# A state-space and MLP block on one core: eight buffers for X, the table spread on VectorE, some normalisations on GpSimd, and a new order of work

## The chip, the core and the metric

The kernel runs on one core of a Trainium2 chip. The metric is the device time of one execution in microseconds (us). A core has five engines with a queue each: TensorE (PE in the profile; its weight loads are PEld), VectorE (DVE), ScalarE (ACT), GpSimd (POOL) and SyncE (SP), which here only starts transfers (DMA). Each engine works through its own instructions in the order in which the program lists them, and waits on semaphores for the others.

## The reference

Sequence 2048, width 512, bf16. Two kinds of layers alternate, A, B, A, B, with the same weights in both rounds:

```python
x = A_q
x = x + A(layernorm(x))      # A: q * y
x = x + B(layernorm(x))      # B normalises its input once more
x = x + A(layernorm(x))
x = x + B(layernorm(x))

# A: k_shift = causal 4-tap filter of k along the sequence; kv = k_shift * v
#    y = long convolution of kv with ssm_k (length 2048, by FFT) + kv * ssm_D
#    result q * y, where q is the normalised x
# B: y = layernorm(x); h = gelu_tanh(y @ w1 + b1); result h @ w2 + b2    (512 -> 1376 -> 512)
```

The convolution's result y depends on k, v and the filter alone, so it is the same in both A layers and is computed once.

## The kernel before

The work falls into two parts. **The front part** computes y as a transform in two stages, written as matmuls with tables, on tiles of 1024 PSUM columns (two banks each):

- *ht*: the filter is loaded in four blocks of 128 channels (512 KB each) and transposed on TensorE, four tiles of 16 transposes, each copied from PSUM to SBUF. ssm_D is added into the first row of each of the four (line 521, VectorE or GpSimd).
- *s2*: a table that comes from memory in two halves (512 KB each) is spread to four times its size by eight multiplications with masks (lines 498 to 503), 128x2048 each. h2 and x2 read the result.
- *h1* and *h2*: the filter's first and second stage, 16 tiles each (lines 534 and 547). h2 needs all of h1. Its result H lies in SBUF, the core's memory, and 16 transfers of 256 KB (line 564) put a copy with exchanged partition halves beside it, HS.
- *fir*: k, brought in by eight transposing transfers, is filtered on TensorE (line 584, 8 tiles) and multiplied with v on VectorE (line 590).
- *x1*, *x2*: the same two stages for kv. x1 has 16 tiles. x2 (`products`, line 598) runs for two halves of the channels, `PARTS`, eight tiles for each half: TensorE's tile of 16 matmuls, a copy of it to a buffer of X in SBUF (line 615), and a multiplication of X with H and HS on VectorE (line 618, 128x2048) that overwrites H and HS.
- *i1*, *i2*: the way back. i1 has 8 tiles for each half (line 634) and needs all eight products of its half; i2 has 5 tiles for each half (line 688) and leaves y.

X has four buffers of 1024 columns, used in turn (lines 612 and 613), in the memory `R_7`, where the transposed k lay before, so that the first of them waits for the last reader of k. The same memory later holds eight buffers for normalised slices (`ntmp`, line 727).

**The back part** works on the sequence in 16 slices of 128 rows, gathered in blocks: in the first round 1, 1, 2, 2, 2, 2, 2, 2, 2 slices (blocks 0 to 8), in the second 4, 4, 4, 4. For each block:

- statistics of each slice on VectorE (line 709, then the aggregate in line 711), a power on GpSimd for the inverse deviation (lines 715 and 717), the first normalisation (`norm`, line 723), the multiplication with y and the addition to x (lines 750 and 751; in the first four slices in two halves of 256 columns);
- the same statistics again, and a second normalisation;
- a transposition of the normalised slice: for slices 0 and 1 of the first round on TensorE (line 769), for all others by a transposing transfer on SP (line 762); the transposed block has two buffers in turn;
- m1, eleven tiles of four matmuls (line 782) and a gelu on ScalarE (line 787); m2, eleven matmuls per slice (line 815, in three groups of 4, 4 and 3), added to x on VectorE (line 819). In the second round the results are stored to memory as they become ready; the last slice is done in three pieces (lines 804 to 810).

**The order** of all this is written out. The program records 1082 operations by their dependences. `ORDER` lists them in the sequence in which they are given to the engines, so that each engine's own sequence is what `ORDER` leaves of it. `SECOND` names those that run on the second of two engines they may run on: copies from PSUM are on ScalarE or VectorE (`BOTH = (ACT, DVE)`), the row adds of ht on VectorE or GpSimd. `BANKS` gives the PSUM banks of each tile. `sync` sets the semaphore waits from the dependences. In the kernel before, VectorE has 357 operations, ScalarE 222, GpSimd 70, SP 89; of the eight spreads seven are on VectorE and one on ScalarE; of the 96 copies from PSUM (front part and transposes of slices 0 and 1) 23 are on VectorE.

Of the kernel before, what the change touches and what calls it, by code (L numbers as in the profile page):

```python
# [7 lines left out]
ALU = mybir.AluOpType  # L8
AF = mybir.ActivationFunctionType
# [3 lines left out]
PE, ACT, DVE, POOL, SP = "tensor", "scalar", "vector", "gpsimd", "sync"  # L13
# [25 lines left out]
class Prog:  # L39
# [48 lines left out]
    SECOND = (  # L88
        31, 32, 33, 34, 35, 36, 37, 43, 46, 47, 49, 50, 53, 55, 67, 75, 77, 79, 81, 89, 99, 101, 107, 109, 139, 143, 165, 175, 183, 209,
        257, 259, 360)  # L90
    BANKS = (
# [7 lines left out]

    def __init__(self, nc):  # L100
        self.nc = nc
# [259 lines left out]
PARTS = ((0, 64), (64, 64))  # L361
# [494 lines left out]
```

## Time and profile before

| | us |
|---|---|
| median of 3 runs | 242.53 (242.35 to 243.30) |
| the profiled execution | 241.77 |
| its span, first to last instruction | 240.0 |
| TensorE busy | 227.0 (95%) |
| VectorE busy | 177.8 (74%) |
| ScalarE busy | 141.1 (59%) |
| GpSimd busy | 33.2 (14%) |

The span and all times inside the kernel are of the one profiled execution, counted from its first instruction. A busy share is an average over parts of the kernel with different limits. Matmuls overlap with one another, so that TensorE's busy time is longer than the sum of what each costs in a dense row: 16 matmuls of x1 start 0.447 us before those of the next tile. The granted clock of TensorE is 1.0 throughout.

In a group's line stand line number, engine, operation, output and input with shapes, count, then busy time and mean ns of one, then the idle time of the engine before them. A timeline line has start, length, engine, line and operation. In a line of the chain of waits: start, length, and the work that the end waited for at that time.

### The profile page before, as it was taken

Reading aid. Unit: us, or ns where it says so; the run is one execution under the profiler, and the core shown is the slowest. Engines: PE = TensorE matmul, PEld = TensorE weight load, DVE = VectorE, ACT = ScalarE, POOL = GpSimd, SP = SyncE. Lnnn points to the kernel's source line nnn. Section 1 sums busy time; section 2 is a strip of 40 time slices with the busy share of each in tenths; the row PEclk is TensorE's granted clock in tenths of the full one; section 3 lists DMA queues with packets and bytes.
Section 4 is the critical chain, followed back from the end, with each engine's and each line's share of the span. In section 5 each row is a group of like instructions: output and inputs, shape, how many; then the busy total and the mean of one; then the engine's idle time right before and its main releaser. Section 6 shows DMA issues by size and latency. Waiting matters only on the chain.

```text
span 240.0 us, 5685 instructions
## 1 busy us (share of the span) xinstructions
PE 227.0 (95%) x2403; PEld 153.5 (64%) x2418; DVE 177.8 (74%) x357; ACT 141.1 (59%) x220; POOL 33.2 (14%) x74
## 2 busy tenths in 40 slices
PE   6897999888999799999999999999999999999995
PEld 2786889777899686767465856754444444444444
DVE  0899899999998999999899999999979231022013
ACT  2698749999989993739334726627406603703810
POOL 1160000100032224133213022030210100000000
PEclk9999999999999999999999999999999999999999
DMA  6999928999910013020601123122062141002002
GB/s 215 335 262 276 183 72 262 288 317 331 391 45 3 0 27 63 6 44 0 90 0 22 25 44 67 25 45 45 19 78 80 22 109 45 2 0 87 0 3 87
DMA packets 41582, 24.09 MB, mean 100 GB/s; under 512 B 27762, under 2 KB 37844, under 8 KB 41556
## 3 DMA queue, kind: packets, MB, share of 16 engines
q1 hardware_dynamic: 40738, 23.57, 37.3%
q8 instruction: 19, 0.31, 0.6%
q10 hardware_dynamic: 818, 0.15, 0.5%
q14 instruction: 7, 0.06, 0.1%
HBM read 11.40 MB, written 2.10 MB: 56 GB/s over the span
## 4 chain that ended last, share of the span: by engine, by line
PE 75%; ACT 9%; DVE 7%; DMA 4%; issue 1%; POOL 1%; SPq 1%
PE ps L815 30%; PE ps L782 30%; ACT ar L450 9%; PE ps L632 6%; DMA ar<-in_A_ssm_k_dram 3%; PE ps L582 3%; PE ps L545 3%; DVE ar L450 3%; PE ps L804 1%; DMA ar<-ar 1%; DVE sm L709 1%; PE ps L686 1%; DVE ar L447 1%; DVE ar L503 1%; SPq L436 1%
## 5 line engine op out<-in xcount | busy, mean ns | idle before, releaser
L787 ACT ACTIVATE ar<-ps,sm 128x256 bf16<-128x256 f32 (+3 forms) x143 | 68.5, 532 | 73.5 <-PE ps L782 73.4
L782 PE MATMUL ps<-ar 128*128 128x256 bf16 (+5 forms) x569 | 81.5, 297 | 1.3 <-ACT ar L787 1.1
L815 PE MATMUL ps<-ar 128*128 128x512 bf16 (+1 forms) x329 | 76.3, 379 | 0.6
L450 ACT ACTIVATE ar<-ps 128x1024 bf16<-128x1024 f32 (+2 forms) x73 | 67.3, 1035 | 11.7 <-PE ps L515 4.2
L782 PEld LDWEIGHTS ps<-ar 128*128 128x128 bf16 (+1 forms) x572 | 53.1, 100 | 28.9 <-DVE sm L709 1.3
L815 PEld LDWEIGHTS ps<-ar 128*128 128x128 bf16 (+1 forms) x341 | 33.3, 98 | 36.7 <-ACT ar L787 0.4
L819 DVE TENSOR_TENSOR ar<-ar,ps 128x512 bf16<-128x512 bf16 x31 | 21.0, 678 | 39.7 <-PE ps L815 39.7
L447 DVE TENSOR_TENSOR ar<-ar 128x512 bf16<-128x512 bf16 (+3 forms) x89 | 46.5, 536 | 2.4 <-ACT ar L450 0.9
L709 DVE BATCH_NORM_STATS2 sm<-ar 128x6 f32<-128x512 bf16 (+1 forms) x68 | 43.2, 649 | 0.9
L723 DVE TENSOR_SCALAR ar<-ar,sm 128x512 bf16<-128x512 bf16 x64 | 24.5, 412 | 5.8 <-POOL sm L717 4.2
L450 DVE CAST ar<-ps 128x1024 bf16<-128x1024 f32 x19 | 22.7, 1213 | 0.4 <-PE ps L545 0.2
L715 POOL TENSOR_SCALAR sm<-sm 128x2 f32<-128x2 f32 (+2 forms) x26 | 5.3, 204 | 116.3 <-DVE sm L711 115.8
L717 POOL TENSOR_TENSOR sm<-sm 128x2 f32<-128x2 f32 (+2 forms) x26 | 20.6, 793 | 2.2
L532 PE MATMUL ps<-ar 128*64 128x128 bf16 x512 | 17.2, 221 | 1.5 <-ACT ar L450 1.0
L532 PEld LDWEIGHTS ps<-ar 128*64 128x64 bf16 x512 | 14.8, 110 | 3.4 <-ACT ar L450 2.0
L632 PE MATMUL ps<-ar 128*128 128x128 bf16 x256 | 15.2, 220 | 0.6 <-ACT ar L450 0.6
L632 PEld LDWEIGHTS ps<-ar 128*128 128x128 bf16 x256 | 14.6, 114 | 0.9 <-ACT ar L450 0.9
L711 DVE BATCH_NORM_AGGREGATE sm<-sm 128x2 f32<-128x6 f32 (+1 forms) x64 | 11.3, 180 | 1.6
L609 PE MATMUL ps<-ar 128*128 128x64 bf16 x256 | 10.9, 199 | 1.7 <-ACT ar L450 1.7
L609 PEld LDWEIGHTS ps<-ar 128*128 128x128 bf16 x256 | 9.6, 118 | 2.9 <-ACT ar L450 2.6
L589 DVE TENSOR_TENSOR ar<-ps,ar 128x1024 bf16<-128x1024 f32 x8 | 9.5, 1220 | 1.1 <-PE ps L582 1.0
L545 PE MATMUL ps<-ar 128*128 128x128 bf16 x128 | 8.7, 221 | 1.3 <-DVE ar L450 1.3
(31 smaller groups left out, 79.1 us busy)
## 6 DMA issues: line engine op xcount, KB each, us to landing
ar<-ar SPq DMA_DIRECT2D x16, 256.0 KB, 5.4
ar<-in_A_ssm_k_dram SPq DMA_DIRECT2D x4, 512.0 KB, 6.4
ar<-in_A_v_dram SPq DMA_DIRECT2D x4, 512.0 KB, 4.6
ar<-in_A_q_dram SPq DMA_DIRECT2D x4, 512.0 KB, 5.4
out_dram<-ar SPq DMA_DIRECT2D x7, 256.0 KB, 2.0
ar<-in_B_w_dram SPq DMA_DIRECT2D x1, 1376.0 KB, 11.9
ar<-in_B_w_dram SPq DMA_DIRECT2D x1, 1280.0 KB, 9.9
ar<-tab_s SPq DMA_DIRECT2D x2, 512.0 KB, 6.5
```

The lines of the kernel that those rows point to most:

```text
L447: return P.op(eng, lambda e: e.tensor_tensor(o, a, b, op), reads=[a, b] + list(more), writes=[o])
L450: f = {ACT: lambda e: e.activation(dst, src(), AF.Copy), DVE: lambda e: e.tensor_copy(dst, src())}
L532: r = e.matmul(Q(tl, 64 * ri, 64, i * 128, [1, 128]), w, m, start=True, stop=True)
L609: r = e.matmul(Q(tl, 0, 128, i * pitch, [1, n]), w, m, start=True, stop=True)
L632: r = e.matmul(Q(tl, 0, 128, i * 128, [1, 128]), w, m, start=q == 0, stop=q == 1)
L709: P.op(DVE, lambda e, sj=sj, x=x: e.bn_stats(sj, x), reads=[x], writes=[sj])
L717: P.op(POOL, lambda e: e.tensor_tensor(r, v, hf, ALU.pow), reads=[v, hf], writes=[r])
L723: P.op(DVE, lambda e: e.tensor_scalar(o, x, m, r, ALU.subtract, ALU.mult), reads=[x, m, r], writes=[o])
L782: r = e.matmul(Q(tl, 0, rows, 0, [1, w]), a, m, start=dk == 0, stop=dk == 3)
L787: P.op(ACT, lambda e, dst=dst, tl=tl, rows=rows, bias=bias, w=w: e.activation(dst, Q(tl, 0, rows, 0, [1, w]), AF.Gelu_apprx_tanh, bias=bia ...
L815: r = e.matmul(Q(tl, 0, 128, 0, [1, 512]), ins[fc][0], ins[fc][1], start=fc == 0, stop=fc == 10)
L819: P.op(DVE, lambda e, x=x, tl=tl: e.tensor_tensor(x, x, Q(tl, 0, 128, 0, [1, 512]), ALU.add), reads=[x], writes=[x], tile=tl)
```

## The change

No operation is added or taken away. Four things change:

1. *X.* Each half has eight buffers of its own, one for each tile, so that none is used twice: the first half's lie in `R_4`, where the filter's first stage (read by h2) lay and later i1's result lies; the second half's in `R_5`, where kv (read by x1) lay and later y lies. X no longer shares memory with the transposed k. `R_7` keeps the transposed k and then the normalised slices.
2. *The spread.* All eight multiplications may run on VectorE alone.
3. *First normalisations of the first round* may run on VectorE or GpSimd. Eight of the 18 are put on GpSimd: those of slices 0 and 1, both of block 2, and one each of blocks 4, 5, 7 and 8.
4. *The order.* `ORDER`, `SECOND` and `BANKS` are replaced as a whole. VectorE now has 350 operations, GpSimd 77, ScalarE 222, SP 89. Copies from PSUM on VectorE: 22 instead of 23; all four of ht, four of h1, four of h2, five of x1, none of x2, three of i1, one of i2, one of the slices' transposes. On SP the four blocks of the filter come first, then the two halves of the table, then k, v and the rest. On TensorE the tiles of m1 and m2 of neighbouring blocks are mixed more than before, and the last twelve groups of matmuls belong to seven slices of the last two blocks.

```diff
     ORDER = (
-        0, 4, 24, 23, 27, 1, 7, 20, 28, 2, 6, 5, 12, 21, 10, 29, 11, 42, 38, 16, 43, 13, 51, 8, 52, 44, 31, 54, 56, 32, 17, 55, 9, 48, 30,
...
+        7, 0, 27, 28, 2, 22, 1, 51, 24, 4, 6, 42, 52, 53, 43, 29, 48, 49, 80, 44, 81, 84, 60, 85, 5, 20, 50, 72, 73, 32, 21, 30, 34, 8, 274,
...
     SECOND = (
-        31, 32, 33, 34, 35, 36, 37, 43, 46, 47, 49, 50, 53, 55, 67, 75, 77, 79, 81, 89, 99, 101, 107, 109, 139, 143, 165, 175, 183, 209,
-        257, 259, 360)
+        43, 44, 46, 49, 52, 53, 61, 65, 67, 69, 87, 93, 113, 115, 139, 141, 143, 163, 165, 251, 253, 261, 292, 305, 348, 360, 393, 398, 503,
+        555, 662, 714)
...
-    R_XB, R_N = R_7, R_7
+    R_N = R_7
+    XB = {PARTS[0][0]: R_4, PARTS[1][0]: R_5}
...
-            P.op(BOTH, {ACT: lambda e, o=o, x=x, w=w: e.activation(o, x, AF.Copy, scale=w),
-                        DVE: lambda e, o=o, x=x, w=w: e.tensor_scalar(o, x, w, None, ALU.mult)}, reads=[x, w], writes=[o])
+            P.op(DVE, lambda e, o=o, x=x, w=w: e.tensor_scalar(o, x, w, None, ALU.mult), reads=[x, w], writes=[o])
...
-            xo = R_XB + (nx[0] % 4) * 1024
-            nx[0] += 1
+            xo = XB[d0] + k0 // nk * 1024
...
-    def norm(s, mr, o):
+    def norm(s, mr, o, eng=DVE):
         x = A(0, 128, R_X + s * 512, [1, 512])
         m, r = mr
-        P.op(DVE, lambda e: e.tensor_scalar(o, x, m, r, ALU.subtract, ALU.mult), reads=[x, m, r], writes=[o])
+        P.op(eng, lambda e: e.tensor_scalar(o, x, m, r, ALU.subtract, ALU.mult), reads=[x, m, r], writes=[o])
...
-                norm(s, mr[i], zt)
+                norm(s, mr[i], zt, DVE if L else (DVE, POOL))
```

96 rows, old and new, of tables (BANKS, ORDER) are left out of this document.

## The prediction

> **What bounds it now.** I read four views in this order: the busy time by stage, the chain that ended last, the groups by shape, and the timeline of one collision. By stage (stretch and its length, then busy us and count on TensorE, its weight loads, VectorE, ScalarE and GpSimd; granted clock, DMA share, GB/s):
>
> ```profile
> 21.40:43.20 21.80, 21.42 (x480) 19.24 (x480) 20.30 (x19) 16.21 (x18) 0.29 (x2) 1.00 0.80 197
> 43.20:61.60 18.40, 15.78 (x368) 13.77 (x368) 18.21 (x20) 18.40 (x22) 0.76 (x2) 1.00 1.06 322
> 61.60:79.40 17.80, 17.80 (x271) 17.14 (x272) 16.73 (x34) 16.63 (x20) 4.29 (x11) 1.00 0.29 113
> 79.40:89.80 10.40, 8.58 (x116) 7.13 (x115) 9.69 (x33) 10.08 (x26) 2.33 (x6) 1.00 0.07 14
> 89.80:237.60 147.80, 147.00 (x843) 83.48 (x856) 98.30 (x240) 65.36 (x125) 19.76 (x37) 1.00 0.19 40
> ```
>
> Up to 43 us TensorE has enough to do, to 61.6 ScalarE is never idle and VectorE hardly, then TensorE again, then a gap at 79 to 90, and from 90 us TensorE is full to the end at full clock. So time can be won only before 90 us, and lost anywhere. The chain says the same (start, length, what):
>
> ```profile
> 17.95 3.40 DVE ar L450 x3
> ...
> 37.61 12.48 ACT ar L450 x14
> ...
> 69.55 5.36 PE ps L632 x96
> ...
> 87.35 2.45 DMA ar<-ar
> ...
> 89.84 2.54 PE ps L815 x11
> ```
>
> First VectorE, then ScalarE copying PSUM, then i1 on TensorE, then the transposing DMA behind a second normalisation, and after it matmuls alone.
>
> Prices by shape (busy, mean ns of one), and the one collision of GpSimd with a normalisation:
>
> ```profile
> L503 DVE TENSOR_SCALAR ar<-ar,sm 128x2048 bf16<-128x2048 bf16 x7 | 5.1, 769 | 0.2 <-DMA ar<-tab_s 0.2
> ...
> L502 ACT ACTIVATE ar<-ar,sm 128x2048 bf16<-128x2048 bf16 x1 | 2.0, 1993 | 0.0
> ...
> L447 POOL TENSOR_TENSOR ar<-ar 128x256 bf16<-128x256 bf16 x4 | 2.8, 696 | 6.2 <-DMA ar<-in_A_shift_k_dram 6.0
> ```
>
> ```profile
> 70.34 0.80 DVE L723 TENSOR_SCALAR ar<-ar,sm 128x512 bf16<-128x512 bf16 x1
> 70.47 0.52 POOL L668 MEMSET ar<- 1x512 bf16 x1
> ```
>
> Sums below use start-to-start spacing in dense stretches of the timeline, which is shorter than the mean duration because neighbours overlap: on VectorE 1.135 us for a 1024-column PSUM copy or a product of X, 0.62 for statistics over 512 columns, 0.14 for their aggregate, 0.33 for a normalisation, 0.43 for a 512-wide add or multiply, 0.66 for a spread; on ScalarE 0.91 for a PSUM copy. TensorE: 0.447 us per tile of h1, x1 and h2, 0.893 per tile of i1, 0.216 per 512-column matmul.
>
> **Start (0 to 21.5 us).** First h2 matmul: now at 21.46. The new order puts the four filter loads ahead of both tables. Now they land at 5.27, 6.58, 9.54 and 10.95 with a table between the second and third; without it the last two move up one slot each, to about 8.2 and 9.5, and the tables to about 11 and 12.4. VectorE then has ahead of the last h1 copy: four transposed-filter copies (4 x 1.15), two row adds (2 x 0.2), five spreads (5 x 0.66) and four h1 copies (4 x 1.135), in all 12.8 us after 6.57, plus about 1 us of waits for the second table and the last transposes: 20.4. ScalarE has lost its spread (1.9) and one filter copy (1.8) and got two more h1 copies (+1.8); its twelve end at about 20.7. First h2 at about 20.9, 0.6 earlier. But three spreads now stand behind the h1 copies (3 x 0.66, to 22.4), and the fourth h2 tile in the new order needs them: it would be ready at 22.2. With the copies behind it, the seventh h2 tile ends near 24.3 and the first fir tile near 25.3, where it ends now (25.25). Worth: nothing at the end of it, bounds -0.6 and +0.3.
>
> **Up to i1 of the second half.** Last fir product: now ends at 38.2; in the new order, with all h2 ahead of the last fir tile, at 39.5 (TensorE: 25.3 plus 9 h2, 7 fir at 0.87, 2 x1 and ten changes of tile shape at the 0.2 us seen now, 38.3; then the product's 1.2). From there to the last product of the second half VectorE has, now, 6 copies, 16 products, 4 statistics, 2 aggregates, a normalisation: 28.1, to 66.3, measured 66.7. New: 5 copies, 16 products, 4 statistics, 4 aggregates: 26.9, to 66.4, with 0.2 of waits 66.6. First i1 tile of that half: 67.1 now, 66.9 then. **Eight buffers** remove a wait that this trace does not show: ScalarE, which fills them, is busy all 18.40 us of the second row, so nothing waited for a fifth buffer. I cost them at 0; the cover is that VectorE's products set the pace, and if they did not, ScalarE's 0.91 against VectorE's 1.135 for eight tiles is 1.8 us at most. R_5 and R_4 are free of their old readers by then (all x1, all h2 done in TensorE's own order). On SP one swap that the second half of the first products needs stands behind fifteen other transfers; issued near 44.6 and landing 2.7 later it is there at 47.3, wanted at 49. That is 1.7 us of cover.
>
> **The gap at 79 to 90 and behind it** decides. From the last product to the last second normalisation of block 4, VectorE has now 17 normalisations, 19 statistics (8 half wide), 16 aggregates, 25 adds and multiplies (16 half wide), 3 copies and small ones: 30.2 us. In the new order: 12 normalisations (five now on GpSimd), 25 statistics, 19 aggregates, 28 adds and multiplies, one i2 copy more: 34.6. The five save 1.6; six statistics (3.7), three multiplies (1.3), three aggregates (0.4) and the copy (0.6) are new before this point. TensorE's work between first i1 of the second half and first m1 of block 4 is 34.7 now and 35.6 then, two m1 tiles more. Measured now: 66.7 + 30.2 = 96.9, but that normalisation ended at 99.7, so 2.8 us are waits (for i2, for GpSimd's powers, for dependent neighbours). TensorE reached block 4 at 105.0 where 67.1 + 34.7 = 101.8: 3.2 idle. New, with the same 2.8: 66.6 + 34.6 + 2.8 = 104.0, DMA 2.45 as in the chain: 106.4. TensorE would be there at 66.9 + 35.6 = 102.5, so 3.9 idle. What comes after is the same work, so the end moves by (66.9 + 3.9) - (67.1 + 3.2) = **+0.5**. Blocks 5 to 8 and the second layer have 0.7 us or more between landing and need by the same sums.
>
> **Normalisations on GpSimd.** No row shows one. From below 0.19 (its tiny TENSOR_SCALAR, in the timeline); nearest, 0.61 for a two-input op over 256 columns undisturbed; from above 2 x 0.94, twice the slowest of those four, which ran beside a spread. On GpSimd's own queue the statistics of block 2 stand behind one and those of block 4 behind another; each has over 2 us to spare, so the length alone costs 0. What it does to VectorE: the normalisation in the last fence took 0.80 instead of 0.41 beside a 0.52 us GpSimd write, 0.39 lost; multiplies beside GpSimd's powers stayed at 0.42. So 0 to 0.94 (the slowest row again) lost for each; I take 0.39, the row of a normalisation. Six of the eight fall before block 4's deadline; two lie beside copies and statistics, one beside m2 adds; three beside products, normalisations and multiplies. 3 x 0.39 = 1.2, less 0.2 slack: **+1.0**, bounds 0 and 5.6.
>
> The Trainium skill (SBUF — State Buffer, "SBUF: two separate sides") says that the port pair that VectorE and GpSimd share is an exclusive lock for a whole instruction and the loser blocks entirely; the 0.39 of 0.52 fits it. Its GPSIMD Engine Reference (3.1) has 769 ns for 512 elements of a tight loop; by that, as an estimate, three blocked instructions would cost 2.3 in place of 1.2.
>
> **Tail.** Now the last matmul ends at 237.58 and the kernel at 240.0. New: four adds of 0.6 to 0.69 fall within TensorE's last 1.3 us, and a 256 KB store (2.0 to landing) goes out after one of them in place of a 32 KB one (1.5). **+0.2**, bounds 0 and 0.6.
>
> Sum 0.5 + 1.0 + 0.2 = +1.7: span 240.0 to 241.7. The profiled execution took 241.77 against a median of 242.53, 0.8 apart; the median moves to **244.2**.
>
> **Rivals.** (1) *Faster.* The added statistics fill VectorE's 2.8 us of waits in place of standing behind them, and GpSimd hinders nobody. Then block 4 is normalised at 101.2, lands at 103.7, and TensorE's idle time is set by blocks 0 and 1. Block 0's i2 copy ends near 77.2, as now (77.3); from there to its transposes it is 2.8 now, one multiply more then: 80.4. Block 1's normalisation follows 1.9 later, its transposes and their copy take 1.5 more: first m1 at 83.9, where TensorE's own work gives 82.1. So 1.8 in place of 3.2. -1.4 - 0.2 + 0.2: 241.1. For it: VectorE idled 0.76 at 77.4 and 0.7 us in the row of the gap. Against: most waits are links of one chain, statistics, power, normalisation, DMA, which other work doesn't shorten. It decides when block 4's data land before 104.3. (2) *The lock in full:* all six GpSimd normalisations stop VectorE for their length, 0.61 each: 3.7 - 0.2 + 0.5 + 0.2 = +4.2: 246.7. For it the collision above; against, copies from PSUM beside GpSimd kept 1.21. (3) *No collision matters, the rest holds:* +0.7: 243.2.
>
> **Chances.** Forecast 0.36, rival 1 0.30, rival 3 0.22, rival 2 0.12. Range 240.3 to 247.2: rival 1 less 0.8, rival 2 plus 0.5; the forecast's own range is 243.2 to 245.4. Half a per cent (1.2 us: below 241.3, above 243.7) is about what can be told from no change. Faster: 0.24 of rival 1 and 0.01 of rival 3, 0.25. Slower: 0.25 of the forecast, 0.04 of rival 3, all of rival 2, 0.41. Same: 0.34.
>
> **What would show it.** First h2 near 20.9 with a wait at the fourth tile; first i1 of the second half near 66.9; first m1 of block 4 waiting for its DMA near 106; products or multiplies lengthened beside GpSimd's 512-wide TENSOR_SCALAR; TensorE full after that. Wrong if i1 of the second half begins before 65.5, if block 4 doesn't wait, or if TensorE idles after 110 us.

## The result and the profile after

| | before | after |
|---|---|---|
| median, us | 242.69 (242.35 to 243.3, 4 runs) | 245.13 (244.97 to 246.0, 4 runs) |
| ratio after to before | | 1.0125, 95% interval 1.0098 to 1.0152 |
| profiled execution, us | 241.77 | 246.0 |
| its span, us | 240.0 | 244.2 |

The changed kernel is slower by about 1.25%, 2.4 us by the medians and 3.0 by the ratio, where the forecast said 0.6 to 0.7%. The profiled execution is the longest of its four; the spans of the other three are 243.2 to 243.4 us. Line numbers after the change are lower by one (norm 722, powers 714 and 716, products 448, copies 451). Operations are named by their numbers in `ORDER`.

Busy time by stage, cut at the first i1 tile of the second half and the first m1 tile of block 4 (stretch, length, then busy us and count of TensorE, weight loads, VectorE, ScalarE, GpSimd; clock, DMA share, GB/s). The kernel before:

```profile
21.40:67.10 45.70, 42.70 (x944) 38.51 (x944) 43.98 (x44) 40.11 (x44) 1.05 (x4) 1.00 0.92 266
67.10:105.04 37.94, 36.03 (x396) 29.05 (x395) 35.16 (x97) 28.71 (x57) 12.09 (x27) 1.00 0.11 24
105.04:237.60 132.56, 131.85 (x741) 73.21 (x752) 84.09 (x203) 57.87 (x107) 14.29 (x26) 1.00 0.18 40
```

and the changed one:

```profile
21.10:69.90 48.80, 42.64 (x944) 38.42 (x944) 44.10 (x45) 42.39 (x47) 18.49 (x11) 1.00 0.89 262
69.90:109.10 39.20, 37.44 (x403) 29.45 (x404) 36.12 (x99) 29.30 (x59) 17.32 (x27) 1.00 0.11 22
109.10:241.30 132.20, 131.70 (x744) 72.15 (x744) 76.28 (x193) 52.30 (x105) 18.59 (x28) 1.00 0.18 37
```

TensorE has the same 944 matmuls in the first stretch and as much busy time, but the stretch is 3.1 us longer. The second is 1.3 longer, with seven matmul records and 1.4 us of TensorE's busy time more, and the third is 0.4 shorter. (Block 4's first matmul starts at 105.25 before and 109.08 after, its first weight load at 105.04 and 109.08; cut at the matmul the second stretch is 1.0 longer.) Most of what is lost is lost before 70 us, where GpSimd is busy 18.5 us instead of 1.1. The chain that ended last (start, length, what) says what the first stretch waited for:

```profile
20.96 6.33 DMA ar<-in_A_v_dram
34.33 2.37 DVE ar L589 x2
...
47.76 9.28 ACT ar L451 x10
...
62.62 7.21 DVE ar L448 x6
69.97 2.85 PE ps L631 x48
...
106.58 2.45 DMA ar<-ar
```

A transfer of v is now one of its longest links; the chain of the kernel before has none. VectorE's waits in the first stage (who, for what: us in all, times, longest), in the kernel before:

```profile
DVE ar L589 <- PE ps L582: 1.0, 3, 0.4
DVE ar L450 <- PE ps L545: 0.2, 1, 0.2
DVE ar L447 <- ACT ar L450: 0.2, 1, 0.2
```

and in the changed one between 20 and 70 us, with GpSimd's below them:

```profile
DVE ar L589 <- DMA ar<-in_A_v_dram: 2.0, 1, 2.0
...
DVE ar L448 <- ACT ar L451: 0.9, 1, 0.9
```

```profile
POOL sm L662 <- DMA ar<-in_B_b_dram: 6.9, 1, 6.9
```

The 2.0 us stand ahead of the first filter product (135), for the v rows of transfer 16, landed at 27.30. Not all of them are the transfer's: the filter tile that 135 also needs ended at 26.00. The 0.9 are put down to ScalarE, which had long been done; what landed then, at 51.23, is swap 126 (one of the transfers that make HS), and product 199, the second of the second transform stage, starts at 51.31. The 6.9 us are GpSimd's: a copy of ten columns of the gelu biases (276) stands at the head of its queue until transfer 275 has landed at 50.60. Behind it are the powers of blocks 0 and 1 and their normalisations.

In the kernel before, 276 stood ahead of the same powers and waited for 275 even longer, but there 275 landed at 40.97, ahead of block 0's statistics, so that it held up nothing. GpSimd in the kernel before:

```profile
41.02 0.19 POOL L663 CAST sm<-ar 128x10 f32<-128x10 bf16 x1 [23.81 <-DMA ar<-in_B_b_dram]
...
43.84 0.19 POOL L715 TENSOR_SCALAR sm<-sm 128x1 f32<-128x1 f32 x1 [2.47 <-DVE sm L711]
```

What moved is the transfer. SP issues it behind 33 others where it was behind 23, at 46.10 us where it was 35.32; the kernel before, then the changed one, whose line has 275 and the transfer behind it:

```profile
35.32 0.62 SPq L436 DMA_DIRECT2D ar<-in_B_b_dram  x1
```

```profile
46.10 1.40 SPq L437 DMA_DIRECT2D ar<-in_B_b_dram  x2
```

So the three late things, v rows, swap and biases, all come from SP's new order. The groups by shape (busy, mean ns of one, idle before):

```profile
L722 DVE TENSOR_SCALAR ar<-ar,sm 128x512 bf16<-128x512 bf16 x56 | 21.5, 413 | 12.6 <-POOL sm L716 10.8
L722 POOL TENSOR_SCALAR ar<-ar,sm 128x512 bf16<-128x512 bf16 x8 | 23.7, 2957 | 1.6 <-DVE ar L448 0.9
```

These eight are half of the first round's sixteen first normalisations (the text on the change says 18). A normalisation that takes VectorE 0.41 us takes GpSimd 2.96 on average: 2.08 at least, 4.67 at most. Three of them lie beside the products of the second stage. GpSimd's timeline, then VectorE's:

```profile
50.66 0.19 POOL L662 CAST sm<-ar 128x10 f32<-128x10 bf16 x1 [6.88 <-DMA ar<-in_B_b_dram]
...
54.19 8.57 POOL L722 TENSOR_SCALAR ar<-ar,sm 128x512 bf16<-128x512 bf16 x2
```

```profile
60.82 0.17 DVE L710 BATCH_NORM_AGGREGATE sm<-sm 128x2 f32<-128x6 f32 x1
60.91 1.62 DVE L448 TENSOR_TENSOR ar<-ar 128x2048 bf16<-128x2048 bf16 x1
```

Two normalisations take 8.57 us there, and three products (205, 230, 236) take 1.62 to 1.63 in place of 1.22.

### The profile page after: what moved, and what is told of

It is laid out like the page before. It is cut to its first block, busy times and chain, and to the rows that moved or that the text cites. A ratio compares the mean times of both kernels' runs of the same rounds, so it can differ in the third digit from the quotient of the medians.

```text
span 244.2 us, 5689 instructions
## 1 busy us (share of the span) xinstructions
PE 228.9 (94%) x2418; PEld 153.4 (63%) x2418; DVE 170.3 (70%) x350; ACT 136.6 (56%) x220; POOL 59.5 (24%) x81
## 4 chain that ended last, share of the span: by engine, by line
PE 60%; DVE 17%; SPq 8%; ACT 6%; DMA 5%; issue 2%; POOL 0%; DVEq 0%
PE ps L814 26%; PE ps L781 26%; DVE ar L448 6%; SPq L470 6%; ACT ar L451 5%; DVE sm L708 4%; PE ps L631 3%; DMA ar<-in_A_v_dram 3%; DVE ar L451 2%; SPq L437 2%; DMA ar<-in_A_q_dram 2%; DVE ar L589 1%; DVE ar L722 1%; PE ps L582 1%; PE ps L545 1%
## 5 line engine op out<-in xcount | busy, mean ns | idle before, releaser
L786 ACT ACTIVATE ar<-ps,sm 128x256 bf16<-128x256 f32 (+5 forms) x143 | 64.9, 532 | 73.6 <-PE ps L781 69.5
L781 PE MATMUL ps<-ar 128*128 128x256 bf16 (+4 forms) x572 | 84.5, 297 | 1.5 <-ACT ar L786 1.1
L814 PE MATMUL ps<-ar 128*128 128x512 bf16 (+1 forms) x341 | 81.1, 379 | 0.0
L451 ACT ACTIVATE ar<-ps 128x1024 bf16<-128x1024 f32 (+2 forms) x74 | 68.5, 1014 | 15.6 <-PE ps L532 7.4
L722 DVE TENSOR_SCALAR ar<-ar,sm 128x512 bf16<-128x512 bf16 x56 | 21.5, 413 | 12.6 <-POOL sm L716 10.8
L722 POOL TENSOR_SCALAR ar<-ar,sm 128x512 bf16<-128x512 bf16 x8 | 23.7, 2957 | 1.6 <-DVE ar L448 0.9
L716 POOL TENSOR_TENSOR sm<-sm 128x2 f32<-128x2 f32 (+2 forms) x26 | 22.9, 880 | 2.2
L451 DVE CAST ar<-ps 128x1024 bf16<-128x1024 f32 (+1 forms) x17 | 19.9, 1182 | 0.7 <-PE ps L532 0.3
L631 PE MATMUL ps<-ar 128*128 128x128 bf16 x256 | 15.2, 219 | 2.2 <-ACT ar L451 1.6
L807 DVE TENSOR_TENSOR ar<-ar,ps 128x128 bf16<-128x128 bf16 (+1 forms) x3 | 1.0, 332 | 19.5 <-PE ps L803 19.4
```

Source lines behind the costliest of these rows:

```text
L451: f = {ACT: lambda e: e.activation(dst, src(), AF.Copy), DVE: lambda e: e.tensor_copy(dst, src())}
L631: r = e.matmul(Q(tl, 0, 128, i * 128, [1, 128]), w, m, start=q == 0, stop=q == 1)
L716: P.op(POOL, lambda e: e.tensor_tensor(r, v, hf, ALU.pow), reads=[v, hf], writes=[r])
L722: P.op(eng, lambda e: e.tensor_scalar(o, x, m, r, ALU.subtract, ALU.mult), reads=[x, m, r], writes=[o])
L781: r = e.matmul(Q(tl, 0, rows, 0, [1, w]), a, m, start=dk == 0, stop=dk == 3)
L786: P.op(ACT, lambda e, dst=dst, tl=tl, rows=rows, bias=bias, w=w: e.activation(dst, Q(tl, 0, rows, 0, [1, w]), AF.Gelu_apprx_tanh, bias=bia ...
```

## The experiments

Ratios are to the kernel before on the same chip, with a 95% interval. Sequences of numbers are one engine's or queue's own, read out of `ORDER`. Transfers 8 and 9 belong to the transposed k (line 469 of the kernel before), although one expectation calls 8 filter rows; 16 to 19 are v.

**a1: the eight normalisations back on VectorE**, order unchanged.

```diff
     SECOND = (
-        43, 44, 46, 49, 52, 53, 61, 65, 67, 69, 87, 93, 113, 115, 139, 141, 143, 163, 165, 251, 253, 261, 292, 305, 348, 360, 393, 398, 503,
-        555, 662, 714)
+        43, 44, 46, 49, 52, 53, 61, 65, 67, 69, 87, 93, 113, 115, 139, 141, 143, 163, 165, 251, 253, 261, 292, 360)
```

> The changed kernel with the eight first normalisations back on VectorE, in the place that the order gives them. Theory A (the loss is late transfers; GpSimd only lengthens three products by 0.41 us each): those three come back to 1.22 (-1.2 us), but VectorE gets six normalisations of 0.33 before block 4 (+2.0), so 0 to +0.8 us against the changed kernel, that is 245.1 to 245.9. Theory B (the GpSimd normalisations, 2.1 to 4.7 us each, are the loss): at least 1.5 us faster than the changed kernel, 243.6 or less. In both no product stays above 1.25 us.

246.58 us, ratio 1.0180 (1.0156 to 1.0204): slower still, and above the range of either theory. The lengthened products are gone, the v wait (2.0 us) is not, and VectorE's third normalisation (393) now stands 1.1 us waiting for GpSimd's power. So taking GpSimd's normalisations out of this order doesn't win the loss back.

**a2: the early transfers in the order in which they are wanted.** On SP the v rows (16) go ahead of k's transfer 9, swaps 126 to 129 ahead of 122 to 124; a small transfer (274) and a table (26) go back.

```diff
-8, 274, 9, 17, 12, 10, 11, 13, 16, 19, 15, 14, 272, 18, 121, 118, 119, 266, 120, 130, 26, 122, 127, 129, 128, 123, 124, 275, 273, 126
+8, 16, 9, 17, 12, 10, 11, 13, 15, 19, 14, 18, 274, 272, 121, 118, 119, 266, 120, 130, 126, 127, 129, 128, 122, 123, 124, 26, 275, 273
```

> The changed kernel with SP's sequence alone altered: the first quarter of v goes out right after the first transposing load of k, and the swap that the second product waited for goes out four places behind the first of its kind in place of nine. Theory A: the wait of 2.0 us of the first fir product for v and the wait of 0.9 us of the second product for the swap go away; the first i1 tile of the second half starts 1.5 to 2.4 us earlier than 69.9 (67.5 to 68.4) and the time falls to 242.7 to 243.6. Theory B: VectorE's work and GpSimd set the pace from there on, so the waits only move; less than 0.5 us is won, 244.6 or more.

245.66 us, ratio 1.0147 (1.0113 to 1.0182): nothing gained that the intervals show. But the first i1 tile of the first half starts at 58.16 us, 2.8 earlier than in the changed kernel; that of the second half starts at 69.34, only 0.6 earlier. VectorE's waits between 45 and 72 us in this kernel (its line 713 is the aggregate, 725 the normalisation):

```profile
DVE sm L713 <- POOL ar L725: 2.6, 1, 2.6
```

Block 2's aggregate (388) writes to the place of the mean that block 0's normalisation (305) still reads. Copy 276 held GpSimd's queue until 49.5 and then itself took 4.8 us, so 305, 2.08 us long, ended at 60.57, and VectorE waited. Behind that, from 68.80 to 72.21 us, TensorE had half its clock in this execution. The three of a2's six executions with that one's mean clock, 0.992 to 0.993, took 246.1 to 246.8 us, the others 244.6 to 245.2. The loss itself isn't this: of the changed kernel's four only the shortest is at 0.993.

**a3: both edits of a1 and a2.**

> Both edits at once. Theory A: within 0.8 us of the run with moved transfers alone, on the slower side. Theory B: 1.5 us or more below it.

246.88 us, ratio 1.0201 (1.0168 to 1.0233). Worse again; its profiled execution also has 60.2 to 67.1 us at half clock, so its stages aren't used.

**b1: the kernel before with eight buffers of X and nothing else.**

```diff
-    R_XB, R_N = R_7, R_7
+    R_N = R_7
+    XB = {PARTS[0][0]: R_4, PARTS[1][0]: R_5}
...
-            xo = R_XB + (nx[0] % 4) * 1024
-            nx[0] += 1
+            xo = XB[d0] + k0 // nk * 1024
```

> The kernel before with eight buffers of X for each half in the new places and nothing else: same order, same engines. Theory A (nothing waited for a fifth buffer, ScalarE was busy without a gap there): within 0.3 us of the kernel before. Rival: the new places make copies wait for the last readers of the filter's first stage or of kv, or free the copies from the readers of k: a change of more than 0.5 us, with a gap in ScalarE between 43 and 61 us.

242.22 us, ratio 1.0008 (0.9991 to 1.0025). In the order of the kernel before the buffers are worth nothing, as costed.

After a2 the theory was: two queues are late in the first stage, SP's and GpSimd's, and mending one only brings the wait to the other.

**c1: the bias copy behind normalisation 393.**

```diff
-303, 276, 346, 278, 304, 347, 305, 348, 391, 392, 393, 277
+278, 303, 346, 304, 347, 305, 348, 391, 392, 393, 276, 277
```

> The changed kernel, with one edit: on GpSimd the small bias copy (operation 276), which in the changed kernel stands ahead of the powers 346, 304, 347 and the normalisations 305, 348 and waits until 50.60 us for its transfer, goes behind normalisation 393. Theory Q (the held GpSimd queue is what costs: everything behind the copy is late): the powers run near 44 to 46 us and the normalisations near 45 to 52, block 0 is ready earlier, and the time falls by 1 us or more, to 244.2 us or less. Theory V (what costs in the first stage is VectorE's idle time ahead of its products, 2.0 us for the v rows and 0.9 us for swap 126; nothing that VectorE does waits for the late normalisations in the changed kernel): the first 64-column tile of the inverse transform still starts at 69.5 to 70.2 us, and the time stays at 244.6 to 245.7 us.

244.66 us, ratio 1.0083 (1.0058 to 1.0109), at the edge of theory V's range; the interval overlaps the changed kernel's, 1.0098 to 1.0152. GpSimd's normalisations 305 and 348 moved to 46.6 and 48.7 us and took 2.1 each, and the first i1 tile of the second half still starts at 69.80. That last number is weak: in c1's profiled execution, the longest of its six, TensorE had half its clock from 60.03 to 63.44 us. In e4 below, which has the same GpSimd order and full clock, that tile starts at 69.09.

**c2: a2 and c1 together.**

> Run a2 (the changed kernel with the order of the early transfers on SP's queue mended) with the bias copy also moved behind normalisation 393 on GpSimd. In a2 VectorE stood idle 2.64 us at the aggregate 388 of block 2, which waited for GpSimd's normalisation 305. If that wait is what ate a2's gain: no idle time over 0.5 us on VectorE between 45 and 65 us, the first 64-column tile at 66.5 to 67.8 us, and 243.0 to 244.2 us. If the gain of the first stage is lost in the later stages whatever the first does: that tile early as said, but the time at 245 us or more. If GpSimd's long normalisations hold VectorE even from their earlier place: idle time of 1 us or more at 388 or 390 again, and 244.4 to 245.5 us.

242.90 us, ratio 1.0022 (1.0006 to 1.0038): the first case, 0.1 us below its range. By the ratios c1 is worth 0.4%, which the intervals don't separate from nothing, a2 nothing, and both together 1.0%, which they do. The waits for the v rows and for the swap are gone from VectorE's list (20 to 70 us):

```profile
DVE ar L592 <- PE ps L585: 2.0, 4, 0.7
DVE ar L454 <- PE ps L548: 0.2, 1, 0.2
```

GpSimd's timeline in c2:

```profile
45.56 4.26 POOL L725 TENSOR_SCALAR ar<-ar,sm 128x512 bf16<-128x512 bf16 x2
...
62.14 4.51 POOL L725 TENSOR_SCALAR ar<-ar,sm 128x512 bf16<-128x512 bf16 x1
```

and its first stretch:

```profile
20.70:66.50 45.80, 42.47 (x944) 38.55 (x944) 43.27 (x45) 41.53 (x46) 12.68 (x9) 1.00 0.90 261
```

45.8 us, as in the kernel before (45.70). The first two normalisations now lie beside copies from PSUM and statistics and take 2.1 each; 393 still lies beside products, takes 4.51, and one product 1.63. Which of a2's moves the gain needs wasn't tried, nor was transfer 275 put back ahead by itself with 276 where it is.

**c3: c2 with the normalisations on VectorE**, and the products in one run: 305, 388, 348, 390 behind the last (copy 251 goes along with them), 393 and 398 ahead of 498. **e3: c3 with 503 and 555 a few places later.**

```diff
-395, 503, 400, 403, 401, 358, 454
+395, 400, 403, 401, 358, 503, 454
...
-504, 460, 555, 602, 463, 655, 465
+504, 460, 602, 463, 655, 465, 555
```

> c2 with the eight first normalisations back on VectorE, and with the 16 products of the second transform stage run without a break there: normalisations 305, 348 and aggregates 388, 390 behind the last product, 393 and 398 ahead of aggregate 498. If the first stage decides (VectorE's idle time and its lengthened products are the loss of the changed kernel): the first 64-column tile starts at 65.5 to 67.0 us and the time is 242.0 to 243.4 us. If the loss is in the later stages of the searched order: the tile starts as early, and the time is 244.4 us or more. In between: both, in the shares that the stage times show.

> c3 (first normalisations on VectorE) with two of them put where their powers are ready: 503 behind 358, 555 behind 465; in c3 VectorE stood idle 1.26 and 1.87 us ahead of them. If c3 is 3.0 us longer than c2 because of these two waits (a place in the order, not the engine): 242.9 to 243.9 us. If it is VectorE's added work (six normalisations by 0.41 us in the stretch up to block 4, where VectorE is busy nearly without a break): 244.8 to 245.9 us. Both: in between.

c3 took 245.89 us (1.0149, 1.0124 to 1.0174), e3 244.62 (1.0099, 1.0080 to 1.0119). c3's first stage is as good as c2's (66.96 against 66.53), but block 4 starts 4.05 us later. VectorE's waits for powers between 66 and 107 us, in c3 and then in e3:

```profile
DVE ar L724 <- POOL sm L718: 3.1, 2, 1.9
```

```profile
DVE ar L724 <- POOL sm L718: 1.3, 2, 1.0
```

It was both: about 1.2 us by the ratios were the two places, and 1.9 us (1.0099 against 1.0022) are left. VectorE's added work is the likely cause, but the other places chosen for the eight weren't tried apart from it. In this order GpSimd's normalisations are a gain over both placements on VectorE.

**d2: the kernel before with the eight normalisations on GpSimd**, order unchanged.

```diff
-        257, 259, 360)
...
+        183, 209, 257, 259, 360, 305, 348, 393, 398, 503, 555, 662, 714)
...
-                norm(s, mr[i], zt)
+                norm(s, mr[i], zt, DVE if L else (DVE, POOL))
```

> The kernel before, its order unchanged, with the eight first normalisations on GpSimd and nothing else. Theory L (the length of a GpSimd normalisation, 2.1 to 4.7 us in the changed kernel, and the VectorE products that it lengthens cost time when the order doesn't allow for them): block 0's blends, which in the kernel before followed normalisation 305 within 9 us, and 348 and 393, are late by 1.7 us each or more: 243.2 to 245.0 us. Rival (the length costs nothing since GpSimd is idle, only the lock costs about 1 us at most): 242.0 to 243.1 us.

250.61 us, ratio 1.0339 (1.0311 to 1.0367), far beyond both. The group on GpSimd, and VectorE's waits from 58 to 112 us (line 723 the normalisation, 447 blends and products, 711 the aggregate); the kernel before has none of these normalisations on GpSimd:

```profile
L723 POOL TENSOR_SCALAR ar<-ar,sm 128x512 bf16<-128x512 bf16 x8 | 17.7, 2215 | 19.7 <-DVE ar L447 19.0
```

```profile
DVE ar L447 <- POOL ar L723: 6.9, 4, 2.3
DVE sm L711 <- POOL ar L723: 2.0, 1, 2.0
```

Five waits, 8.9 us, against 8.2 us lost by the ratio and 9.4 by the spans. Where the next work on VectorE needs the normalisation, each wait is about 2 us, the normalisation's own length (2.2 on average here).

**e1: c2 with the tail mended**, the last product of slice 10 ahead of the last group of slice 7, with its addition and its transfer; **f3: the same edit in the changed kernel alone.**

```diff
-1073, 1068, 1069, 1070, 990, 1076
+1073, 990, 1068, 1069, 1070, 1076
```

> c2 with the last product of output slice 10 (990), its addition 991 and its transfer 996 put ahead of the last group of slice 7 (1068 to 1071, 1072), as it is done earlier in the kernel before. If the tail of the changed kernel is longer because the transfer of a full slice (996) is issued last: from the last matmul to the end of the span 2.3 to 2.5 us where c2 shows 2.92 us, and 242.2 to 242.6 us. If the transfers at the end set the tail whatever their order: 2.8 us or more, and 242.8 to 243.0 us.

> The changed kernel with the tail of e1 and nothing else (990, 991, 996 ahead of the last group of slice 7). If the tail costs the changed kernel what e1 against c2 showed (ratio 0.9998 against 1.0022), whatever its first stage does: 244.3 to 244.8 us, and 2.3 to 2.6 us from the last matmul to the end of the span instead of 2.92. If the order of the first stage is all of the loss and e1's gain was scatter: 244.9 to 245.5 us.

e1 took 242.21 us, ratio 0.9998 (0.9984 to 1.0013); from last matmul to end 2.58 us where c2 has 2.92. f3 took 245.43, ratio 1.0133 (1.0111 to 1.0155), with 2.60 us at the end. The tail is shorter by 0.3 us in both traces; f3's time doesn't show it, and the intervals of e1 and c2 overlap, so that the other half of e1's 0.6 us isn't shown to be more than scatter.

**e2: e1 with copy 296 ahead of the first gelu**, statistic 655 ahead of 463 and blend 351 behind 312.

```diff
-286, 317, 288, 333, 321, 329, 296, 339
+286, 317, 288, 296, 333, 321, 329, 339
```

> e1 with three more places changed between 80 and 92 us: on ScalarE copy 296 goes ahead of gelu 333, into 1.3 us in which ScalarE stands idle; on VectorE statistic 655 goes ahead of square sum product 463, which waits 1.04 us for a power, and blend 351 behind aggregate 312. In c2 TensorE stands idle 1.00 us (83.8 us) and VectorE 0.92 us (85.2 us) for that copy. If VectorE's chain sets the start of block 4: block 4's first tile 1.2 to 1.9 us earlier against the start of the 64-column inverse tiles than in c2, and 240.8 to 241.6 us. If TensorE's idle time only moves to the next wait: 0.5 us or less, 242.0 us or more.

242.60 us, ratio 1.0013 (0.9998 to 1.0027): no gain, the second case. The idle 1.3 us of ScalarE weren't idle. ScalarE's timeline in c2:

```profile
80.52 1.51 ACT L454 ACTIVATE ar<-ps 128x512 bf16<-128x512 bf16 x2 [0.76 <-PE ps L771]
82.05 1.28 ACT L789 ACT_TABLE_LOAD   x1
83.34 0.88 ACT L789 ACTIVATE ar<-ps,sm 128x128 bf16<-128x128 f32 x3
```

A table load stands ahead of the first gelu and moves with it; in e2 TensorE's weight loads waited 1.8 us for that gelu instead of 0.9.

**e4: c1 with the v rows moved alone** on SP.

```diff
-8, 274, 9, 17, 12, 10, 11, 13, 16, 19
+8, 16, 274, 9, 17, 12, 10, 11, 13, 19
```

> c1 (changed kernel, bias copy behind) with one transfer moved on SP's queue: the v rows (16) go behind the filter rows 8, the rest as in the changed kernel. In c1 VectorE stood idle 2.0 us for the v rows and 1.37 us for swap 126 at 50.8 us. If the two waits lie in series and the second takes up what the first gives: VectorE's wait ahead of the first filter product falls to 0.7 us, its wait ahead of the second product of the second stage (199) grows to 2 us or more, and the time stays at 244.2 to 244.9 us. If each costs by itself: 243.0 to 243.7 us.

245.09 us, ratio 1.0120 (1.0098 to 1.0142), nothing gained. The v rows were there early (landed at 14.60 and 18.98), but VectorE still waited 1.4 us ahead of product 135, now for TensorE's filter tile:

```profile
DVE ar L592 <- PE ps L585: 2.7, 4, 1.4
```

In this execution the first h2 tile came at 21.83, 1.0 us later than in c1, and the first filter tile ended at 27.41, as late as the v rows had been in the changed kernel (27.30). So what the v rows cost by themselves isn't told by this run. (c1's own wait for them was 1.4 us; the 2.0 of the expectation is the changed kernel's.) What holds is that 199 starts at 51.28, as swap 126 lands (51.20), just as in the changed kernel (51.31): at that product the swap decides.

**f1: e1 with the preload of the gelu table first on ScalarE; f2: the kernel before with the same move.**

```diff
-0, 2, 1, 81, 85
+0, 2, 1, 3, 81, 85
```

> e1 with one operation moved: ScalarE's preload of the gelu table (operation 3) goes from its place near 106 us to the front of ScalarE's order, behind its three transfer issues. In e1 the trace shows a table load of 1.28 us at 82.22 us, directly ahead of the first gelu, and one at 2.21 us ahead of the first copy; TensorE stands idle 1.00 us (83.9 us) for the first gelus. If the first load can be that of the gelu table and the copies need no other: no load at 82 us, the first gelu 1.3 us earlier, TensorE's idle time there 0.3 us or less, and 241.0 to 241.7 us. If the copies load their own table anyway, or the idle time moves to block 4: 242.0 to 242.5 us.

> The kernel before with the same single move of operation 3. It too shows 1.31 us between the last copy and the first gelu (at 83.54 us), and 1.36 us in which TensorE waits at 84.3 us, but later it waits for VectorE's chain ahead of block 4's neighbours. If the load is on the path in both kernels: 241.0 to 241.7 us, and the comparison of the mended changed kernel with it stays at no difference. If in the kernel before VectorE's chain hides it: 241.9 to 242.5 us.

f1 took 240.96 us, ratio 0.9950 (0.9932 to 0.9968): faster than both kernels. ScalarE's timeline there has no load at 82 us; the only one, at 2.21, belongs to the preload, and the copies need no other:

```profile
80.77 1.51 ACT L454 ACTIVATE ar<-ps 128x512 bf16<-128x512 bf16 x2 [0.75 <-PE ps L771]
82.17 0.89 ACT L789 ACTIVATE ar<-ps,sm 128x128 bf16<-128x128 f32 x3
```

From the first i1 tile of the second half to block 4 it takes 38.1 us, 1.1 less than c2. f2 took 242.22, ratio 1.0007 (0.9991 to 1.0023): between the first i1 tile of the second half and block 4 TensorE is 0.6 us quicker, and then its weight loads wait 0.7 us at 108.9 for an addition on VectorE. So the load isn't part of what the change lost; it is a gain that the mended new order takes and the order before doesn't.

## Why the prediction was right and wrong

The direction was right and the time inside the range, the median of 245.13 even inside the forecast's own 243.2 to 245.4. The size was off: +1.7 forecast for the span, +4.2 measured in the profiled execution, about +3 by the ratio. That the median lies so near is luck, since no term of the sum stands for the late transfers. Its terms one by one:

- **Start, 0: nearly.** h2 began at 21.17 (20.9 forecast) and its fourth tile waited 0.5 us for a spread, as said, but the first fir tile ended at 26.00, 0.5 later than before (25.49), where the bound was 0.3.
- **Up to i1 of the second half, 0.2 earlier: this is the step that failed.** It began 2.8 us later than before (69.93 against 67.10). VectorE's work was forecast well: it is busy 57.6 us up to there, 58.3 before. The waits weren't: its idle time is 12.3 us, 8.8 before, where the step had given them 0.2 us. Three things make them up. The v rows weren't looked at, though SP's order has transfer 16 behind fourteen others, where it was behind nine; VectorE waited 2.0 us, and the last fir product ended at 40.95, where 39.5 was forecast and c2 has 39.15. The swap that was to be there at 47.3 with 1.7 us of cover landed at 51.23, and VectorE waited 0.9: it was issued at 47.54, not 44.6, and took 3.7 us, not 2.7. (2.7 was the shortest of the sixteen swaps of the kernel before; their median from issue to landing was 5.4.) And three products were longer by 0.41 each, which the sum has under the lock. They add up to more than 2.8 since they overlap. c2 shows that this stage is what was lost: with SP's and GpSimd's queues mended it is 45.8 us long again and the ratio falls from 1.0125 to 1.0022.
- **Eight buffers, 0: right** (b1, 1.0008).
- **Block 4: right in kind.** By the prediction's own count TensorE idled 3.6 us where 3.9 was forecast (3.2 before), and block 4's weight loads waited 0.4 us for its transfer, landed at 109.03. What the step didn't see is what makes up the idle time: about 1 us of it stands behind a table load (f1).
- **The lock, +1.0: the size right, its reasons not.** Three lengthened instructions by 0.39 were forecast, three by 0.41 came. But a GpSimd normalisation was bounded by 1.88 us and takes 2.08 to 4.67, and "the length alone costs 0" holds only where the order leaves room for it: in d2 it cost 8.9 us of waits. (The 2.6 us of a2 came from a late start, not from length.) In the changed kernel's own trace VectorE never waits for a GpSimd normalisation. The Trainium skill (GPSIMD Engine Reference, 3.1) has 769 ns for 512 elements of a tight loop. The trace has 2.08 us for this operation undisturbed, and the three products lost 1.2 us and not the 2.3 that were worked out from that page. The Trainium skill (SBUF — State Buffer, "SBUF: two separate sides") has the loser of the shared port pair blocked for a whole instruction. The traces agree in part: GpSimd lost up to 2.6 us of one instruction beside a row of products, but a product lost 0.41 us, far less than the 2.08 of the instruction beside it. In the collision that the prediction shows, VectorE's instruction started first (70.34 against 70.47) and was still the one to be longer, so that this row doesn't fit the rule as well as was said.
- **Tail, +0.2: within its bounds.** 2.92 us after the last matmul in place of 2.40: +0.5, bound 0.6.
- **Rivals.** None came true: block 4's data landed at 109.03, not before 104.3, no VectorE instruction stopped for a whole GpSimd one, and the loss is larger than the +0.7 of the third. The signs of being wrong asked only whether i1 of the second half begins too early; it began late.

What the sum missed altogether is GpSimd's queue: a ten-column copy ahead of five operations that others need waits for a transfer that SP now issues 10.8 us later. The prediction had asked what stands behind the normalisations, not what stands ahead of them and when its transfer lands.

The account of the 1.25%: 1.0 for the two queues, shown by c2. Of the rest the traces give the tail 0.3 us, 0.1%; what is left lies within the intervals. What the spread on VectorE alone is worth wasn't tried by itself.

## What to carry to other kernels

When an order is rewritten, walk each in-order queue by itself, the transfers' and the slow engine's too, and write down for every operation that waits for a transfer when that lands and who stands behind it: an operation that kept its place can still be late because its transfer moved, and where two queues are late, mending one can show little (a2, c1) and both together nearly all (c2). Work moved to an idle engine is free only where the order leaves the longer time for it: the same eight operations on GpSimd were 1.9 us better than the best placement on VectorE that was tried in one order, and cost 8 us in another. A gap of constant length ahead of an instruction that moves with it is work, not idle time.

## What was unexpected of the hardware

- GpSimd's 128x512 normalisation took 2.08 us with no product beside it and 3.5 to 4.7 beside two-input bf16 products of VectorE. Beside each of the three in the changed kernel one product lengthened by 0.41; beside the one of 3.46 us in c1 none did. Even a ten-column copy on GpSimd took 4.82 us in place of 0.19 beside such products (a2).
- ScalarE's first gelu cost one load of 1.28 us, and 1.31 from the end of the copy ahead of it to the gelu's start (c2). The Trainium skill (ScalarE: Activation LUTs, "What ACT_TABLE_LOAD costs") has the same 1283 ns and about 1380 more for a drain, 2.66 in all; the drain isn't in this trace. That the copies ran without a load of their own (f1) agrees with its section "Table sets: the hidden batching unit", by which cheap functions, copy among them, are in every set.
- TensorE's granted clock fell to half for 3.4 us behind a stretch of little work in the profiled executions of a2, c1 and f3, and for 6.8 us in a3. In the 3.4 us ahead of it TensorE had been busy 1.2 (a2), 1.7 (c1), 1.6 (f3) and 2.1 us (a3), so it wasn't idle. The rows of c1: 1.5 us with 0.21 us of work, then half clock; i1 tiles took 1.7 us there instead of 0.9.

```profile
58.50:60.00 1.50, 0.21 (x7) 0.10 (x4) 1.50 (x3) 1.50 (x3) 0.00 (x0) 1.00 1.05 342
60.05:63.35 3.30, 3.25 (x31) 3.28 (x32) 3.30 (x5) 2.58 (x3) 1.89 (x2) 0.50 0.96 330
```

The changed kernel has the same stretch (59.40 to 60.96, 0.25 us of work) and no fall behind it, while f3, the same kernel up to its tail, has one. By the Trainium skill (TensorE: Matmul & The Clock Gate, Part 1) the window of 3.4 us runs freely. That a fall comes in one execution and not in the other agrees with that; no run here shows the window itself.
